# A new order table for a fused recurrent-attention and feed-forward kernel on one core

## Chip, core and metric

The kernel runs on one core of a Trainium2 chip. The metric is the time of one execution in microseconds. An order table fixes what each engine does and in which order, and the change replaces that table.

## What is computed

The inputs r, k and v have 4 batches, 8 heads, 768 positions and 48 values per head; w and u have one row per head. Everything comes in and goes out as 32-bit floats.

```
for t in range(S):
    cur     = einsum('bhd,bhe->bhde', u * k[t], v[t])
    y[t]    = einsum('bhd,bhde->bhe', r[t], state + cur)
    state   = w * state + einsum('bhd,bhe->bhde', k[t], v[t])
x   = y, heads side by side            # 3072 x 384
out = relu(x @ w_in) ** 2 @ w_out      # 384 x 2048, then 2048 x 384
```

## The kernel before

The 768 positions are cut into 6 chunks of 128, and a unit is one chunk of one batch: 24 units, numbered 0 to 23, four to a chunk. Within a chunk the recurrence is done as masked attention, and a state of 48 x 48 per head is carried from chunk to chunk. The feed-forward part then takes the 128 rows of a unit.

A unit passes through these steps. The names are those of the order table, and the line numbers are those that the profile shows.

- Loads: `rt`, `kt` (L278, or L281 for half loads) and `vt` or `vtS` (L311 on GpSimd, L309 on SyncE). Units 0 to 5 load r and k in halves of 96 KB and v on GpSimd's queue; from unit 6 on, one load of 384 KB serves two units and all are on SyncE's queue.
- `scale` (L301, L303, VectorE) multiplies r and k by powers of w into the tile rkw. `vb` (L316, L318, ScalarE) casts v.
- The transposes of r and k: up to unit 5, `turn` on TensorE (L333) and `rkT` on ScalarE (L337); from unit 6 on, `rkD` (L322), one transpose by DMA on SyncE for two units. `kb` and `kbT` (L345, L349) turn k back for the state in the first units.
- `rk` (L357, L360), `d` (L389) and `dv` (L420) make the diagonal part with u. `at` (L369) makes r times k, and `mask` (L377) evicts it. `s` (L398, L410), `sadd` (L424), `sdec` (L428) and `stb` (L432) carry the state.
- `y` (L441, L447) and `yb` (L456) make the rows of y. Up to unit 5 `xturn` and `xT` (L477, L481) transpose them for the feed-forward part, from unit 6 on `xD` (L467), a transpose by DMA on SyncE for two units.
- `m1` (L493), `relu` (L501), the squares `sqA` (L508, ScalarE) or `sqD` (L510, VectorE), `m2` in quarters (L517, and L533 in halves for unit 23), `osb` (L524) and the store `out` (L553, L549) are the feed-forward part. Units 0 to 5 do m1 in four steps of 12 matmuls; from unit 6 on a pair of units does it in eight steps of 6 wider matmuls.

The weights come in quarters on GpSimd's queue, `I` (L288) and `O` (L291). `ids`, `upper`, `zeros`, `uwb` and `wend` are small jobs of GpSimd; `wend` waits for `end` on ScalarE. `lnat`, `log`, `w`, `wk`, `wr`, `cols` and `copied` prepare the powers of w. `fill.N` is N warm-up matmuls (L216) that compute nothing that is used.

The tile framework schedules nothing itself here. The string ORDER is walked word by word, and each word emits one step into the queues of the engines that it uses. Each engine and each DMA queue then works through its own words in this order and waits, at the head of the queue, for what the next one needs. The number behind @ is the bank of PSUM that the step's result takes.

```python
for word in ORDER.split():
    what, _, where = word.partition("@")
    name, *a = what.split(".")
    ...
    if where:
        place.update(zip(names(name, *a), (int(x) for x in where)))
    steps[name](*a)
```

SyncE issues every load of r and k but one, v from unit 6 on, both kinds of DMA transposes and all stores, one behind the other.

Of the kernel before, what the change touches and what calls it, by code (L numbers as in the profile page):

```python
# [22 lines left out]
scale.3.0 relu.0.3 wend xturn.1@7 rk.2 at.2@26 xT.1 kb.2@0 mask.2.1 sqA.0.0 kt.5.0 d.2@4 turn.3.0@3 vt.3 s.0@7  # L23
sadd.1 rkT.3.0 m1.0.2@1 kt.5.1 scale.3.1 kbT.2 O.0 m1.1.0@6 mask.2.0 vb.2 relu.0.2 vt.4 turn.3.1@3 dv.2 m1.1.3@5
rt.6 rkT.3.1 sadd.0 O.1 y.2@1 relu.1.0 kt.6 m1.1.2@0 yb.2 relu.1.3 vt.5 at.3@72 rk.3 relu.1.2 kb.3@4 mask.3.1
xturn.2@6 sqA.1.0 O.2 m1.0.1@5 scale.4.0 xT.2 s.2@0 O.3 sqD.0.3 d.3@2 relu.0.1 m1.1.1@1 vb.3 mask.3.0 turn.4.0@3
kbT.3 m1.2.0@6 scale.4.1 relu.1.1 dv.3 m1.2.1@4 rkT.4.0 sqD.1.3 sqA.0.2 y.3@7 m1.2.2@1 scale.5.0 relu.2.1 sqD.1.1
m1.2.3@2 relu.2.2 sqD.0.1 s.3@5 sqA.1.2 turn.4.1@4 m2.0.0@3 sadd.3 relu.2.3 sadd.2 m2.1.0@1 rkT.4.1 yb.3 relu.2.0
m2.1.1 rk.4 vb.4 scale.5.1 kb.4@7 stb.1 xturn.3@6 at.4@42 kbT.4 m2.0.1 mask.4.1 xT.3 stb.0 s.4@5 mask.4.0 turn.5.0@6
m1.3.0@2 sqD.2.1 rkT.5.0 y.4@0 dv.4 relu.3.0 turn.5.1@6 rt.8 sadd.4 m1.3.3@7 rkT.5.1 yb.4 m2.1.2 sqA.3.0 sqA.2.0  # L30
m2.0.2 kt.8 xturn.4@2 m2.0.3 xT.4 scale.6.0 kb.5@5 osb.0 m2.1.3 scale.7.0 relu.3.3 m1.3.1@2 vtS.6 kbT.5 vb.5
m1.4.0@6 scale.6.1 scale.7.1 at.5@75 relu.4.0 m2.2.0@0 mask.5.0 osb.1 rkD.6 sqA.4.0 m1.4.1@4 sqD.2.3 sqA.2.2 sqD.3.3
m1.4.2@1 relu.3.1 mask.5.1 m2.2.1 stb.3 sdec.4 m1.4.3@6 relu.4.2 rt.10 rk.5 y.5@5 sqA.4.2 scale.8.0 s.5@2 scale.8.1
relu.4.1 m2.2.2 scale.9.0 relu.4.3 vtS.8 m1.3.2@1 sqD.3.1 stb.4 m2.3.0@4 dv.5 relu.3.2 yb.5 m2.2.3 scale.9.1 kt.10
m2.3.1 osb.2 sadd.5 sqA.4.1 m2.4.0@1 sqD.4.3 vb.6 xturn.5@0 sdec.5 at.6@2376 xT.5 rk.6 rkD.8 m2.4.1 stb.2 mask.7.0
stb.5 m1.5.0@0 sqA.3.2 mask.6.0 s.7@7 relu.5.0 mask.7.1 m1.5.3@5 mask.6.1 s.6@2 relu.5.3 m2.4.2 dv.6 out.0 vb.8
y.6@3 dv.7 rt.12 y.7@0 yb.6 m1.5.1@6 yb.7 m2.3.2 sadd.6 relu.5.1 xD.6 scale.10.0 m2.4.3 sqA.5.0 scale.10.1 sqA.5.1
m2.3.3 sadd.7 vtS.10 osb.4 m1.5.2@6 scale.11.1 scale.11.0 m2.5.0@3 relu.5.2 sqD.5.3 kt.12 m2.5.1 sqA.5.2 rk.8
at.8@1520 osb.3 sdec.6 m2.5.2 mask.9.0 rkD.10 m2.5.3 mask.8.0 s.8@4 mask.8.1 osb.5 s.9@2 m1.6.0@7 mask.9.1 m1.6.1@6
sadd.8 relu.6.0 dv.9 kt.14 m1.6.3@5 relu.6.1 dv.8 m1.6.7@1 sqA.6.0 scale.12.0 sadd.9 sqA.6.1 y.9@3 rt.14 y.8@4 vb.10  # L40
m1.6.2@0 yb.8 stb.6 m1.6.5@2 yb.9 relu.6.3 sdec.9 xD.8 m1.6.4@6 relu.6.5 scale.12.1 m2.7.0@3 relu.6.2 sqD.6.3
relu.6.7 vtS.12 m2.6.0@4 scale.13.0 relu.6.4 scale.13.1 m1.6.6@7 sqA.6.2 rk.10 at.10@6120 sqA.6.4 rkD.12 m2.6.1
relu.6.6 mask.10.0 sqA.6.5 s.10@5 sdec.7 m2.7.1 sqA.6.6 sqD.6.7 m2.7.2 stb.7 mask.10.1 stb.9 out.1 m2.7.3 sadd.10
kt.16 mask.11.0 y.10@6 osb.7 m1.8.0@1 dv.10 m1.8.1@2 rt.16 scale.14.0 relu.8.0 sdec.8 m1.8.3@5 relu.8.1 mask.11.1
m2.6.2 stb.8 yb.10 sqA.8.1 s.11@3 y.11@2 relu.8.3 dv.11 m1.8.6@1 vb.12 yb.11 m1.8.4@6 relu.8.6 sadd.11 xD.10 m2.6.3
rk.12 sqA.8.0 relu.8.4 scale.15.0 m1.8.2@2 scale.14.1 m1.8.5@0 relu.8.2 sdec.10 out.4 m2.9.0@7 osb.6 scale.15.1
vtS.14 sqA.8.2 sqD.8.3 m2.8.0@6 relu.8.5 out.3 at.12@4312 sqA.8.6 rkD.14 s.12@0 sqA.8.5 mask.13.0 m2.8.1 sqA.8.4
mask.12.1 m1.8.7@5 mask.12.0 m1.10.1@1 relu.8.7 mask.13.1 out.2 m1.10.3@3 relu.10.1 scale.16.0 vtS.16 s.13@4 sadd.12
y.12@2 dv.12 rt.18 m2.8.2 sdec.11 m1.10.6@5 yb.12 m1.10.5@0 dv.13 relu.10.6 sqD.8.7 y.13@2 stb.10 m2.9.1 relu.10.5
scale.17.0 yb.13 sqA.10.6 m2.8.3 sadd.13 relu.10.3 xD.12 m1.10.2@0 osb.8 sqD.10.3 sqA.10.1 m1.10.0@3 scale.16.1  # L50
kt.18 m1.10.7@1 relu.10.0 scale.17.1 rt.20 at.14@5642 relu.10.2 rk.14 sqA.10.0 m2.9.2 mask.15.1 vb.14 m2.9.3
mask.14.0 rkD.16 relu.10.7 m1.10.4@2 mask.14.1 sqA.10.2 mask.15.0 s.15@5 stb.11 s.14@0 sqA.10.5 m2.11.0@3 dv.14
osb.9 y.14@4 relu.10.4 y.15@6 kt.20 yb.14 vb.16 m2.11.1 sdec.12 sqA.10.4 m2.10.0@1 sadd.15 stb.12 out.5 dv.15
m1.12.0@2 sqD.10.7 m1.12.1@7 relu.12.0 yb.15 m1.12.3@4 scale.18.0 xD.14 scale.18.1 m2.10.1 relu.12.3 scale.19.0
m1.12.7@6 relu.12.1 rt.22 m2.10.2 relu.12.7 out.7 m1.12.2@7 sqA.12.0 vtS.18 sqD.12.7 m2.11.2 sdec.13 relu.12.2
scale.20.0 m1.12.6@2 sqA.12.1 kt.22 sadd.14 m1.12.4@7 scale.19.1 m1.12.5@4 scale.21.0 relu.12.4 scale.20.1 m2.11.3
relu.12.5 sqD.12.3 m2.13.0@6 sqA.12.4 rk.16 rkD.18 osb.11 at.16@4705 scale.21.1 sqA.12.2 m2.10.3 mask.16.1 relu.12.6
m1.14.7@3 sdec.15 osb.10 scale.22.0 stb.13 m2.13.1 sqA.12.5 mask.16.0 m1.14.0@7 out.10 relu.14.7 mask.17.0 out.6
s.16@2 relu.14.0 scale.23.0 m2.13.2 out.8 sqA.12.6 mask.17.1 s.17@4 rkD.20 m1.14.2@7 dv.16 sadd.16 m2.12.0@0
relu.14.2 sadd.17 m2.13.3 sdec.14 m2.12.1 dv.17 osb.13 stb.15 y.16@1 out.13 vb.18 y.17@7 yb.16 m1.14.1@6 yb.17  # L60
m2.12.2 scale.22.1 relu.14.1 xD.16 sqD.14.7 m2.12.3 sqA.14.1 scale.23.1 m1.14.6@3 sqA.14.0 rk.18 vtS.20 m1.14.3@1
relu.14.6 rkD.22 at.18@6725 osb.12 stb.14 s.18@4 mask.18.1 sqA.14.2 m1.14.5@3 relu.14.3 mask.19.0 m2.15.0@0
relu.14.5 sqD.14.3 m1.14.4@7 sqA.14.5 mask.18.0 vtS.22 m2.14.0@3 relu.14.4 dv.18 out.9 m2.15.1 mask.19.1 sqA.14.4
s.19@7 sqA.14.6 rk.20 m2.14.1 sdec.17 y.19@1 dv.19 stb.17 y.18@2 m2.14.2 yb.18 m1.16.0@6 yb.19 sadd.19 xD.18
m1.16.4@2 relu.16.0 sdec.16 m2.14.3 sadd.18 relu.16.4 out.11 m1.16.1@1 osb.14 vb.20 at.20@7256 m1.16.3@4 sqA.16.4
mask.20.1 stb.16 m1.16.2@3 rk.22 relu.16.3 m2.15.2 mask.21.1 relu.16.1 relu.16.2 s.20@4 m2.15.3 dv.20 sqA.16.1
m1.16.5@1 mask.20.0 sqA.16.2 sdec.18 m1.16.7@2 sqA.16.0 mask.21.0 relu.16.5 s.21@7 m1.18.7@6 sdec.19 relu.16.7
s.22@3 sqD.16.3 m1.18.3@1 sqA.16.5 osb.15 m1.18.1@2 vb.22 y.20@4 relu.18.1 m1.16.6@0 yb.20 relu.18.3 y.21@5 dv.21
relu.16.6 m1.18.4@4 sqD.16.7 stb.18 m2.17.0@1 yb.21 relu.18.4 dv.22 m2.16.0@0 xD.20 relu.18.7 sqA.18.1 m2.17.1
sqA.16.6 at.22@3567 out.12 out.15 m1.18.6@4 mask.22.0 out.14 m1.18.2@2 mask.22.1 relu.18.6 m2.17.2 mask.23.0  # L70
relu.18.2 mask.23.1 m2.16.1 stb.19 sqD.18.7 y.22@4 m2.16.2 s.23@2 m1.18.5@7 dv.23 m1.18.0@5 sqD.18.3 yb.22 m2.16.3
relu.18.0 m1.20.0@3 sqA.18.4 relu.18.5 m1.20.3@5 osb.16 m1.20.6@2 relu.20.3 out.16 y.23@6 sqA.18.0 sqD.20.3 m2.17.3
sqA.18.5 yb.23 m1.20.7@4 sqA.18.6 xD.22 sqA.18.2 m1.20.1@7 relu.20.7 m1.20.5@5 relu.20.0 sqD.20.7 m2.18.0@0
relu.20.6 m2.18.1 relu.20.5 sqA.20.6 m2.18.2 sqA.20.0 m2.19.0@5 m2.19.1 m1.20.2@4 m1.20.4@3 relu.20.2 m1.22.6@6
sqA.20.2 m1.22.3@4 relu.20.1 relu.20.4 m2.19.2 osb.17 m2.18.3 sqA.20.5 relu.22.6 m1.22.1@3 relu.22.3 m1.22.0@2
sqA.20.1 sqD.22.3 m2.19.3 relu.22.0 m1.22.7@1 osb.19 sqA.22.0 m2.21.0@2 sqA.20.4 m2.21.1 relu.22.1 m1.22.2@7
# [546 lines left out]
```

## Time and profile before

| what | value |
| --- | --- |
| median of 3 runs | 171.85 us (170.75 to 172.5) |
| the profiled execution | 171.94 us |
| its span | 170.2 us, 4733 instructions |
| busy: TensorE, VectorE, ScalarE, GpSimd | 163.9, 122.3, 129.8, 15.7 us |
| DMA | 28.86 MB, mean 170 GB/s |
| granted TensorE clock, mean | 0.988 |

The span runs from the first instruction to the last, and the execution's own time holds 1.7 us more. A row of the groups gives a line, an engine, an operation, output and inputs, the count, busy time, the mean of one in ns and the idle time before them. In rows by time the first number is the start in us from the beginning of the span, the second the length. In the rows by stretch each engine's busy us and instruction count are followed by the granted clock, the mean busy share of the 16 DMA engines (it can pass 1, since their packets overlap) and GB/s. A row of one step's line on SyncE gives the shortest, median and longest hold of the queue in ns and the first and last start; the row below it gives the time from issue to landing.

### The profile page before, as it was taken

To read this page: it belongs to the slowest core of one execution; us is meant where nothing else is said; L and a number is where in the kernel's file an instruction comes from. 1 tells how busy PE (TensorE), PEld (TensorE's weight loads), DVE (VectorE), ACT (ScalarE), POOL (GpSimd) and SP (SyncE) were. 2 spreads that over 40 slices of the span, in tenths; PEclk is the share of its full clock that TensorE was granted. 3 is DMA by queue.
4 is the path that set the end of the run, shared out by engine and by line. 5 is a ranking of instruction groups with operands and counts; after the bars stand their busy time and mean duration, and the time that the engine had idled before them with its cause. 6 is when DMAs were issued, how large, how long until landed. Compare 5 with 4: busy or idle time off the path is not lost.

```text
span 170.2 us, 4733 instructions
## 1 busy us (share of the span) xinstructions
PE 163.9 (96%) x1947; PEld 134.1 (79%) x1947; DVE 122.3 (72%) x243; ACT 129.8 (76%) x255; POOL 15.7 (9%) x36
## 2 busy tenths in 40 slices
...
PEclk9996999999999999999999999999999999999999
DMA  3999999999999899999999997998990501100044
GB/s 92 172 279 240 272 194 254 213 201 227 185 181 218 153 214 190 181 212 191 236 182 202 174 251 173 188 288 197 180 232 4 179 6 54 42 0 4 0 164 162
DMA packets 91493, 28.86 MB, mean 170 GB/s; under 512 B 82864, under 2 KB 90672, under 8 KB 91472
## 3 DMA queue, kind: packets, MB, share of 16 engines
...
q10 hardware_dynamic: 432, 0.25, 0.6%
...
HBM read 20.50 MB, written 4.72 MB: 148 GB/s over the span
## 4 chain that ended last, share of the span: by engine, by line
PE 87%; DMA 6%; DVE 3%; SPq 2%; issue 1%; DVEq 0%
PE bank L493 36%; PE bank L517 34%; DMA rt<-in_r_dram 4%; PE bank L369 4%; PE bank L441 3%; DMA xT<-yb 2%; PE bank L398 2%; PE bank L447 2%; SPq L281 2%; PE bank L533 2%; PE bank L333 1%; PE bank L410 1%; PE bank L345 1%; PE bank L216 1%; PE bank L477 1%
## 5 line engine op out<-in xcount | busy, mean ns | idle before, releaser
L493 PE MATMUL bank<-xT,w_in_q 128*128 128x256 bf16 (+1 forms) x720 | 72.6, 251 | 0.1
L501 ACT ACTIVATE gr<-bank 128x512 f32<-128x512 f32 x96 | 55.3, 604 | 19.0 <-PE bank L493 15.2
L517 PE MATMUL bank<-w_out_q,g 128*128 128x384 bf16 x368 | 68.6, 326 | 0.0
L493 PEld LDWEIGHTS <-w_in_q 128*128 128x128 bf16 x720 | 63.8, 113 | 3.9 <-DMA xT<-yb 0.3
L517 PEld LDWEIGHTS <-g 128*128 128x128 bf16 x368 | 34.3, 98 | 18.1 <-issue 0.2
L508 ACT ACTIVATE g<-gr 128x512 bf16<-128x512 f32 x68 | 41.2, 636 | 0.2
L377 DVE TENSOR_TENSOR am<-bank,smask 128x512 bf16<-128x512 f32 x48 | 31.3, 684 | 7.4 <-PE bank L369 6.6
L510 DVE TENSOR_TENSOR g<-gr 128x512 bf16<-128x512 f32 x28 | 19.0, 686 | 17.2 <-ACT gr L501 17.2
L524 ACT COPY osb<-bank 128x384 f32<-128x384 f32 x23 | 11.0, 480 | 5.7 <-PE bank L517 5.6
L456 DVE TENSOR_TENSOR yb<-bank,dv 128x384 bf16<-128x384 f32 x24 | 12.9, 553 | 3.2 <-PE bank L447 2.3
L420 DVE TENSOR_TENSOR dv<-vb,bank 128x384 f32<-128x384 bf16 x24 | 13.0, 548 | 2.2 <-PE bank L410 1.4
L432 ACT CAST stb<-st 128x384 bf16<-128x384 f32 x20 | 10.2, 522 | 0.6 <-DVE st L428 0.6
L301 DVE TENSOR_TENSOR rkw<-rt,wpos 128x384 bf16<-128x384 f32 x18 | 9.8, 551 | 0.8 <-DMA rt<-in_r_dram 0.7
L301 DVE TENSOR_TENSOR rkw<-kt,wneg 128x384 bf16<-128x384 f32 x18 | 9.7, 551 | 0.8 <-DMA kt<-in_k_dram 0.8
L337 ACT COPY rkT<-bank 128x512 bf16<-128x512 bf16 x12 | 7.0, 590 | 3.4 <-PE bank L333 3.4
L216 PE MATMUL bank<-warm 128*128 128x128 bf16 x87 | 8.4, 265 | 1.1 <-DVE warm L161 1.1
L441 PE MATMUL bank<-vb,am 128*128 128x48 bf16 x192 | 8.9, 185 | 0.0
L428 DVE TENSOR_TENSOR st<-st,wend 128x384 f32<-128x384 f32 x16 | 8.8, 550 | 0.0
L424 DVE TENSOR_TENSOR st<-bank,st 128x384 f32<-128x384 f32 x16 | 8.7, 549 | 0.0
L441 PEld LDWEIGHTS <-am 128*128 128x128 bf16 x192 | 7.9, 97 | 0.8
L369 PE MATMUL bank<-rkT 64*128 64x128 bf16 x192 | 8.2, 221 | 0.2 <-ACT rkT L337 0.2
L216 PEld LDWEIGHTS <-warm 128*128 128x128 bf16 x87 | 7.0, 121 | 1.2 <-DVE warm L161 1.0
...
## 6 DMA issues: line engine op xcount, KB each, us to landing
...
```

The costliest lines, as they stand in the source:

```text
L216: nc.tensor.matmul(out=banks[0][:, :128], lhsT=warm, rhs=warm, start=True, stop=True)
L301: nc.vector.tensor_tensor(t["rkw"][:, x, :, :, :D], pair(src), pair(wneg if x else wpos), ALU.mult)
L369: nc.tensor.matmul(out=t["at"][o][:, p, :], lhsT=t["rkT"][sl, 1, p, :], rhs=t["rkT"][sl, 0, p, :], start=True, stop=True,)
L377: nc.vector.tensor_tensor(am, t["at"][o], smask.unsqueeze(1).to_broadcast([C, HP, C]), ALU.mult)
L420: nc.vector.tensor_tensor(t["dv"], t["vb"], t["d"].unsqueeze(2).to_broadcast([C, H, D]), ALU.mult)
L441: nc.tensor.matmul(out=y[:, 2 * p + o, :], lhsT=t[f"am{o}"][:, p, :], rhs=t["vb"][:, 2 * p + o, :], start=(o == 0 and p == 0), stop=c == 0 ...
L456: nc.vector.tensor_tensor(t["yb"], t["y"], t["dv"].rearrange("p h d -> p (h d)"), ALU.add)
L493: nc.tensor.matmul(out=t["h", s][:, a], lhsT=turned, rhs=chunks[c]["xT"][:, b : b + m, n, :], start=(n == 0), stop=(n == NK - 1),)
L501: nc.scalar.activation(t["gr", s], t["h", s], AF.Relu)
L508: nc.scalar.activation(g, x, AF.Square)
L510: nc.vector.tensor_tensor(g, x, x, ALU.mult)
L517: nc.tensor.matmul(out=t["o"], lhsT=chunks[units[i][0]]["g"][:, f, units[i][1], :], rhs=w_out_q[f // 4][:, f % 4, :], start=(f == 0), stop ...
```

## The change

Only the string ORDER differs. Both lists hold the same steps, 882 words with the fills; the sum of the fills is 93 in the place of 87. Nearly every word is moved, over the whole span, and nearly every bank number is another. The table was searched again with a planner that takes, for how long a transpose by DMA holds SyncE, the times in the trace. The beginning and the end of the diff:

```diff
-kt.0.0 kt.0.1 rt.0.0 rt.1.0 I.0 rt.1.1 vt.0 ktA.1.0 lnat.0 fill.26 log@4567 kt.1.1 lnat.1 ids rt.2.0 w.1 upper w.0
-fill.8 cols@1 rt.2.1 wk scale.0.0 kt.2.0 zeros scale.0.1 wr fill.8 turn.0.0@2 kt.2.1 copied uwb turn.0.1@5 rkT.0.0
-rt.3.0 rkT.0.1 vt.1 rk.0 fill.10 at.0@63 scale.1.0 rt.3.1 I.3 kb.0@4 mask.0.0 d.0@2 turn.1.0@7 I.2 kbT.0 kt.3.0
-mask.0.1 rkT.1.0 vt.2 scale.1.1 vb.0 I.1 kt.3.1 fill.19 turn.1.1@4 dv.0 y.0@3 rkT.1.1 rt.4.0 yb.0 vb.1 rk.1 fill.9
-kb.1@4 kt.4.0 scale.2.0 at.1@31 xturn.0@6 rt.4.1 mask.1.1 d.1@5 turn.2.0@2 xT.0 rkT.2.0 scale.2.1 kt.4.1 fill.5
-m1.0.0@7 kbT.1 mask.1.0 turn.2.1@2 relu.0.0 dv.1 rt.5.0 fill.2 y.1@1 rkT.2.1 m1.0.3@4 yb.1 end rt.5.1 s.1@5
...
+kt.0.0 kt.0.1 rt.0.0 rt.1.0 I.0 rt.1.1 ids ktA.1.0 lnat.0 fill.26 log@4567 kt.1.1 vt.0 lnat.1 rt.2.0 w.1 upper w.0
+rt.2.1 wk scale.0.0 kt.2.0 zeros scale.0.1 wr fill.20 turn.0.0@1 kt.2.1 cols@3 rkT.0.0 turn.0.1@6 copied uwb rkT.0.1
+kt.3.0 rk.0 I.3 fill.9 at.0@32 kb.0@5 rt.3.0 vt.1 mask.0.1 d.0@6 scale.1.0 vt.2 mask.0.0 fill.14 turn.1.0@2 rt.3.1
+I.2 vb.0 kt.3.1 scale.1.1 rkT.1.0 I.1 fill.13 y.0@1 kt.4.0 dv.0 kbT.0 fill.1 turn.1.1@3 vt.3 yb.0 rt.4.0 rkT.1.1 end
+scale.2.0 fill.9 xturn.0@2 O.0 at.1@43 kt.4.1 xT.0 rk.1 fill.1 turn.2.0@1 mask.1.1 vt.4 d.1@6 m1.0.0@2 rkT.2.0
+rt.4.1 scale.2.1 O.1 mask.1.0 m1.0.3@5 vb.1 kt.5.0 relu.0.0 turn.2.1@1 dv.1 wend y.1@7 vb.2 kb.1@0 kt.5.1 yb.1 s.0@4
...
-m2.23.0@0 out.20 m2.22.3 out.19 osb.23.0 out.17 m2.23.1@1 osb.22 out.23.0 out.22 osb.23.1 out.23.1
...
+m2.22.3 m2.23.1@4 osb.22 out.22 osb.23.1 out.23.1
```

SyncE's queue from unit 6 on, taken out of the two tables:

```
before: rt.6 kt.6 rt.8 kt.8 vtS.6 rkD.6 rt.10 vtS.8 kt.10 rkD.8 out.0 rt.12 xD.6 vtS.10 kt.12 rkD.10 kt.14 rt.14 xD.8
        vtS.12 rkD.12 out.1 kt.16 rt.16 xD.10 out.4 vtS.14 out.3 rkD.14 out.2 vtS.16 rt.18 xD.12 kt.18 rt.20 rkD.16
        kt.20 out.5 xD.14 rt.22 out.7 vtS.18 kt.22 rkD.18 out.10 out.6 out.8 rkD.20 out.13 xD.16 ...
after:  rt.6 kt.6 kt.8 rt.8 out.0 vtS.6 rkD.6 rt.10 kt.10 rkD.8 vtS.8 rt.12 out.1 xD.6 kt.12 vtS.10 rkD.10 rt.14 xD.8
        out.2 vtS.12 out.5 kt.14 rkD.12 rt.16 vtS.14 xD.10 kt.16 rkD.14 vtS.16 kt.18 xD.12 rt.18 kt.20 out.4 rkD.16
        rt.20 vtS.18 xD.14 rt.22 out.3 out.7 kt.22 rkD.18 out.6 rkD.20 xD.16 ...
```

Around the first m1 step of each chunk of the middle, TensorE's words are also set otherwise: between at.16 and the end, for one, the new list has 41 paired m1 steps and 48 quarters of m2, the old one 40 and 44.

GpSimd's queue begins `I.0 ids vt.0` in the place of `I.0 vt.0 ids`, has I.3 ahead of vt.1, and has wend behind O.1 and no longer ahead of vt.3. ScalarE has vb.0 ahead of rkT.1.0, and end ahead of xT.0.

More of the change, by code (lines that the diff above doesn't have):

```diff
@@ L22 @@
-m1.0.0@7 kbT.1 mask.1.0 turn.2.1@2 relu.0.0 dv.1 rt.5.0 fill.2 y.1@1 rkT.2.1 m1.0.3@4 yb.1 end rt.5.1 s.1@5
[L23 to L76, printed above, removed]
@@ new lines @@
+kt.3.0 rk.0 I.3 fill.9 at.0@32 kb.0@5 rt.3.0 vt.1 mask.0.1 d.0@6 scale.1.0 vt.2 mask.0.0 fill.14 turn.1.0@2 rt.3.1
+I.2 vb.0 kt.3.1 scale.1.1 rkT.1.0 I.1 fill.13 y.0@1 kt.4.0 dv.0 kbT.0 fill.1 turn.1.1@3 vt.3 yb.0 rt.4.0 rkT.1.1 end
+scale.2.0 fill.9 xturn.0@2 O.0 at.1@43 kt.4.1 xT.0 rk.1 fill.1 turn.2.0@1 mask.1.1 vt.4 d.1@6 m1.0.0@2 rkT.2.0
+rt.4.1 scale.2.1 O.1 mask.1.0 m1.0.3@5 vb.1 kt.5.0 relu.0.0 turn.2.1@1 dv.1 wend y.1@7 vb.2 kb.1@0 kt.5.1 yb.1 s.0@4
+rkT.2.1 vt.5 sadd.0 kbT.1 xturn.1@3 rt.5.0 kb.2@1 rk.2 xT.1 at.2@62 scale.3.0 O.3 kbT.2 mask.2.1 m1.1.0@3 relu.0.3
@@ new lines @@
+rt.5.1 mask.2.0 m1.1.3@1 O.2 relu.1.0 scale.3.1 y.2@2 sqA.1.0 rt.6 d.2@7 turn.3.0@5 dv.2 s.1@4 m1.0.2@0 rkT.3.0
+sadd.1 kt.6 relu.1.3 turn.3.1@7 yb.2 m1.1.2@3 relu.0.2 xturn.2@6 s.2@2 m1.0.1@1 xT.2 scale.4.0 rkT.3.1 m1.2.0@0
+sqD.0.3 sqA.0.0 sadd.2 at.3@65 sqA.0.2 turn.4.0@4 sqD.1.3 relu.1.2 m1.1.1@7 rk.3 relu.0.1 m1.2.1@2 mask.3.1 relu.2.0
+scale.4.1 m1.2.3@1 rkT.4.0 mask.3.0 relu.2.1 m2.0.0@3 sqD.0.1 vb.3 turn.4.1@5 kb.3@6 rkT.4.1 d.3@0 y.3@2 m2.1.0@4
+dv.3 relu.1.1 yb.3 kb.4@5 kbT.3 m1.2.2@0 scale.5.1 sqA.1.2 sqD.1.1 at.4@76 relu.2.3 xturn.3@2 kbT.4 scale.5.0 m2.0.1
@@ new lines @@
+xT.3 mask.4.0 m2.1.1 stb.0 mask.4.1 relu.2.2 turn.5.0@1 turn.5.1@2 vb.4 rk.4 m1.3.1@7 rkT.5.0 y.4@6 kt.8 vb.5 s.4@5
+relu.3.1 s.3@1 m1.3.2@0 sadd.4 sqA.2.0 sadd.3 m2.1.2 relu.3.2 dv.4 rt.8 m2.1.3 rkT.5.1 sqD.2.1 stb.3 m2.0.2 rk.5
+sqA.2.2 yb.4 m2.0.3 stb.1 scale.6.0 xturn.4@0 scale.7.0 m1.3.3@7 osb.0 xT.4 out.0 kb.5@1 scale.6.1 stb.2 m2.2.0@3
+kbT.5 vtS.6 scale.7.1 at.5@25 m1.3.0@1 rkD.6 mask.5.0 m2.2.1 sqD.3.1 relu.3.0 sqD.2.3 m2.2.2 relu.3.3 osb.1 mask.5.1
+s.5@0 sqA.3.0 m1.4.0@2 sadd.5 m1.4.1@1 scale.8.0 relu.4.0 rt.10 scale.8.1 y.5@6 relu.4.1 dv.5 m1.4.3@5 scale.9.0
```

47 lines of the change are left out of this document (45 added, 2 removed).

## The prediction

> **What bounds the kernel now.** I read the page first, then busy time by stretch, then the table of waits, then the chain that ended last, and last SyncE's issues one by one.
>
> ```profile
> PE 163.9 (96%) x1947; PEld 134.1 (79%) x1947; DVE 122.3 (72%) x243; ACT 129.8 (76%) x255; POOL 15.7 (9%) x36
> ...
> PEclk9996999999999999999999999999999999999999
> DMA  3999999999999899999999997998990501100044
> GB/s 92 172 279 240 272 194 254 213 201 227 185 181 218 153 214 190 181 212 191 236 182 202 174 251 173 188 288 197 180 232 4 179 6 54 42 0 4 0 164 162
> ```
>
> Two resources are full at once: TensorE in every slice after the start, and the DMA engines in nearly every slice from the second to the thirtieth (about 126 us). The stretches say it more sharply:
>
> ```profile
> 10.00:20.00 10.00, 9.05 (x148) 8.29 (x149) 8.60 (x17) 6.20 (x15) 3.10 (x6) 0.83 1.15 244
> 70.00:80.00 10.00, 10.00 (x122) 8.41 (x121) 8.59 (x17) 8.88 (x17) 0.00 (x0) 1.00 1.01 204
> ```
>
> TensorE loses time before 20 us alone: it idles 0.95 us of that stretch and its granted clock is 0.83. At 70 to 80 us it is busy throughout, beside a DMA share of 1.01. The table of waits has only scraps for TensorE after the start:
>
> ```profile
> POOL wend L268 <- ACT wend_c L263: 6.9, 1, 6.9
> ...
> PEld L493 <- DMA xT<-yb: 0.3, 1, 0.3
> ...
> PEld L369 <- DMA rkT<-rkw: 0.2, 1, 0.2
> ```
> ```profile
> L322 SPq DMA_TRANSPOSE rkT<-rkw x9: 2171/3824/4443, 38.5 to 117.5; - x9
> ```
>
> So a transpose never held TensorE up for more than 0.3 us, though each rkD holds SyncE for 2.2 to 4.4 us (min, median and max in the last row): what the new order was searched for costs TensorE next to nothing in the old one. The chain gives the price of each TensorE step and the end:
>
> ```profile
> 76.81 3.79 DMA xT<-yb
> 80.65 1.50 PE bank L493 x12
> ...
> 91.35 0.19 PE bank L398 x4
> 91.54 0.65 PE bank L517 x4
> 92.19 0.20 PE bank L441 x8
> 92.39 0.17 PE bank L447 x4
> ...
> 102.72 0.55 PE bank L369 x16
> ...
> 143.16 1.97 PE bank L493 x18
> ...
> 166.43 0.91 PE bank L533 x16
> ```
>
> A paired m1 step (6 matmuls) costs 0.66 us, an m2 quarter 0.65, a y step 0.37 (8 and 4 matmuls), an s step a little over 0.19; at.16 starts at 102.7. The last matmul ends at 167.3; 2.9 us of last eviction and store close the span, and 1.7 us lie outside it (171.94 for this execution, 0.1 above the median of the runs). The chain passes through one transfer behind a full TensorE: xD.10, issued at 76.81, landed at 80.6, and m1.10.1 started with it.
>
> **What the change can touch.** It adds no instruction but six warm-up matmuls (93 for 87):
>
> ```profile
> L216 PE MATMUL bank<-warm 128*128 128x128 bf16 x87 | 8.4, 265 | 1.1 <-DVE warm L161 1.1
> ```
>
> Six of them are 0.6 us at that row's rate. All stand ahead of m1.0.0, where TensorE waits for loads and evictions, so I cost them at nothing; without that cover it is the 0.6. Everything else is moved, on all five queues. With TensorE full after the start, a new order can win only at the start, and it loses wherever TensorE comes to ask for a transfer sooner than the DMA engines bring it.
>
> **The start.** TensorE, VectorE, ScalarE and GpSimd, in turn:
>
> ```profile
> 10.74 0.40 PE L333 MATMUL bank<-identb,rkw 128*128 128x128 bf16 x4 [1.84 <-DVE rkw L303]
> ...
> 16.26 0.83 PE L493 MATMUL bank<-xT,w_in_q 128*128 128x128 bf16 x12
> ```
> ```profile
> 10.13 0.56 DVE L303 TENSOR_TENSOR rkw<-rt,wfour 128x384 bf16<-128x384 f32 x1 [1.63 <-DMA rt<-in_r_dram]
> 10.60 1.28 DVE L377 TENSOR_TENSOR am<-bank,smask 128x512 bf16<-128x512 f32 x2
> ...
> 13.37 0.56 DVE L456 TENSOR_TENSOR yb<-bank,dv 128x384 bf16<-128x384 f32 x1 [0.56 <-PE bank L441]
> ```
> ```profile
> 11.18 0.59 ACT L337 COPY rkT<-bank 128x512 bf16<-128x512 bf16 x1 [1.84 <-PE bank L333]
> 11.66 0.52 ACT L318 CAST vb<-vt 128x384 bf16<-128x384 f32 x1
> 13.05 0.59 ACT L337 COPY rkT<-bank 128x512 bf16<-128x512 bf16 x1 [0.88 <-PE bank L333]
> ...
> 15.73 0.48 ACT L481 COPY xT<-bank 128x384 bf16<-128x384 bf16 x1 [1.68 <-PE bank L477]
> ```
> ```profile
> 3.72 0.96 POOL L311 DMA_DIRECT2D vt<-in_v_dram  x1
> ...
> 18.61 0.99 POOL L268 COPY wend<-wend_c 64x192 f32<-64x192 f32 x2 [6.86 <-ACT wend_c L263]
> ```
>
> The load that both orders wait for (scale.1.0 starts at 10.13) is not moved. Of the two masks that followed it the new list does mask.0.1 inside the 1.63 us wait, so mask.0.0 ends 0.6 us sooner. Against that, vt.0 goes behind the identities on GpSimd, about 0.9 us, and vb.0 now stands ahead of rkT.1.0 on ScalarE: rkT.1.0, kbT.0 and rkT.1.1 queue behind that load, and at.1 waits for the first and the last. vt.0 was there by 11.66. Its landing moves by 0 to 0.9 us; it follows I.0 through the same queue in both orders, so I take none and put vb.0 at 11.6 to 12.1. Then, with the durations above, rkT.1.0 ends at 12.7, kbT.0 at 13.2, rkT.1.1 at 13.8, y.0 at 12.5, dv.0 and yb.0 at 13.6, xturn.0 at 14.0 (the list now puts it ahead of at.1, and moves kb.1 behind m1.0.0), and xT.0, behind two small activations of 0.4, at 14.7. That is the lower bound for m1.0.0, all on time. The upper one is 15.9: turn.1.1 to d.1 took from 12.40 to 16.26 at the low clock, less the 0.4 by which kb.1 goes. I take the middle, **15.3, 1.0 us early**; by m1.1.0 about 0.4 of it is gone again, because vb.1, vb.2 and relu.0.0 (0.5 to 0.6 each) now stand ahead of xT.1 on ScalarE. TensorE's own end moves from 167.3 to **166.7**, with bounds of 165.7 and 167.3.
>
> By the Trainium skill (TensorE: Matmul & The Clock Gate, Part 1: The HAM clock gate) the array runs at half clock by default and after an idle window of some 3.4 us, at full clock after a busy one. The 0.83 above agrees with a gate of that kind. If the 14 fills that now stand ahead of turn.1.0 keep that window busy, this rule would give the early bound, an end near 165.7, in place of 166.7.
>
> **The transfers.** SyncE's rkD.6, rkD.8, rkD.10 and rkD.16, each with its issue and its time to landing, and the xD group:
>
> ```profile
> L322 SPq DMA_TRANSPOSE rkT<-rkw x1: 4115/4115/4115, 38.5 to 38.5; - x1
> DMA to landing us min/median/max: 5.5/5.5/5.5
> ...
> L322 SPq DMA_TRANSPOSE rkT<-rkw x1: 3600/3600/3600, 48.0 to 48.0; - x1
> DMA to landing us min/median/max: 5.1/5.1/5.1
> ...
> L322 SPq DMA_TRANSPOSE rkT<-rkw x1: 4443/4443/4443, 58.3 to 58.3; - x1
> DMA to landing us min/median/max: 7.7/7.7/7.7
> ...
> L322 SPq DMA_TRANSPOSE rkT<-rkw x1: 3824/3824/3824, 93.4 to 93.4; - x1
> DMA to landing us min/median/max: 6.6/6.6/6.6
> ```
> ```profile
> L467 SPq DMA_TRANSPOSE xT<-yb x9: 1211/1262/3002, 53.0 to 143.3; - x9
> ```
>
> They land at 44.0, 53.1, 66.0 and 100.0. An xD that nothing holds up costs 1.2 us (min and median of its row); an rkD turns 16 blocks to its 6, so 3.2. Between the first two landings stand three loads and one rkD: 9.1 less 3.2 leaves 2.0 for a load of 384 KB. A store has 192 KB, so at most 1.0; at the best slice of the page's last row (288 GB/s) it would be 0.7, which I take, since its rows are long. As a test, from 44.0 to xD.10 the old queue has 11 loads, 3 rkD, 3 xD and 2 stores: 22.0 + 9.6 + 3.6 + 1.4 = 36.6, so 80.6, which is where it landed. The transfers are a chain as full as TensorE's, and what is put ahead of a transpose delays it by its price.
>
> Now the new queue. Up to xD.10 it has the same 11 loads (kt.16 is moved behind it, vtS.14 ahead), the same transposes, but four stores: out.0 ahead of vtS.6 and rkD.6, then out.1, out.2 and out.5, where the old one had out.0 and out.1. That is 2 x 0.7 = 1.4 more: xD.10 lands at 82.0. TensorE needs it for m1.10.1, which stood 86.7 us ahead of the end (80.65 to 167.3); behind it the new list has the same 56 m1 steps, 57 m2 quarters and 5 at, one y and one s fewer, 0.6 us: 86.1. **So the end is 82.0 + 86.1 = 168.1**, and m1.10.1, ready at 166.7 - 86.1 = 80.6, waits 1.4 us. A second place says nearly the same: up to rkD.16 both queues have 16 loads and 5 stores, so it still lands at 100.0, but at.16 now has 4 m2 quarters and one m1 step more behind it, 64.6 + 3.3 = 67.9, and 100.0 + 67.9 = 167.9. The other transposes have 0.5 us or more to spare by the same count (rkD.8 and rkD.12 over a microsecond in the old order), and vtS.8, moved behind rkD.8, delays the cast vb.8 but not past s.9. Outer bounds: at 1.0 a store the end is 168.7; if a queue of this kind runs ahead of the sum, TensorE's 166.7 stands.
>
> **Sum.** 168.1 for 167.3 is 0.7 to 0.8 us on the span; with the tail and the time outside unchanged, 171.94 + 0.7 = **172.6 us**, 0.8 above the median shown and inside the 1% that a measurement of this kernel can tell from no change (its three runs lie 1.0% apart).
>
> **The rivals.**
> - *The transfers give way, the start's gain stays* (faster). The holds of SyncE leave gaps in the DMA engines, which an order that knows them may close; the wait at m1.10.1 goes and the end is TensorE's own 166.7: 171.3, at the early bound 170.3. For it: the late transposes of the old run (rkD.20 on) are not needed at once. Against: the share of 1.01 in the middle.
> - *xD.10 lags behind its sum* (slower). rkD.10 landed at 66.0, where the sum (44.0 + 6 loads, 2 rkD, one xD, one store = 20.3) gives 64.3: 1.7 late, and nobody waited but for 0.2 us. With the slack now spent, the same lag on xD.10 or rkD.16 goes to the end in full: 83.7 + 86.1 = 169.8, or 174.4. It makes the run slower by over 1% from a lag of 1.0 us on.
> - *GpSimd's queue crowds out SyncE's loads* (slower). wend moves behind O.1, and end to before xT.0, so the 6.9 us in which GpSimd waited go, and vt.3, O.0, vt.4 and O.1 are issued from about 12 instead of 19.6. The share of 1.15 says that the DMA engines are full there, so the half loads of units 4 and 5 lose what GpSimd gains. If they come 3.4 us later, half of the 6.9, and 1.4 of it is covered, turn.4.0 and turn.5.0 wait 2.0: 168.7, or 173.3; with all of it, 176.8. By the Trainium skill (DMA: Bandwidth & Descriptors, Queues, rings and completion order) each DMA engine takes turns between the queues that have work, packet by packet, which speaks for this loss; no row above separates the two queues.
>
> **How the numbers follow.** The forecast (172.0 to 173.4) has 0.42, the faster rival 0.20, the lag 0.26, the crowding 0.12. Over 1% slower (173.6 on) are the lag, half of the crowding and the top of the forecast's own spread: 0.40. Over 1% faster (170.1 or less) needs the early bound and no wait at all: 0.06. The rest, 0.54, is within 1%. The range leaves out the fastest of the second case and the worst of the last two: 171.0 to 175.0.
>
> **What would show it.** Right: m1.0.0 starts near 15.3; TensorE has its first wait of over a microsecond for xT<-yb near 81 us, or for rkT<-rkw near 100; the page's chain has DMA in it there; VectorE and ScalarE totals stay. The step on the start is wrong if m1.0.0 starts after 16.3 or before 14.7; the step on the stores, if xD.10 lands before 81 with its four stores ahead; the crowding shows as TensorE waits between 22 and 33 us on rkw L303. A run under 170.5 or over 175 would mean that neither chain is what sets the end.

## The result and the profile after

The changed table takes 173.42 us in the median of 12 runs (172.09 to 177.53), the old one 171.20 (170.66 to 172.50): a ratio of 1.011, with an interval of 1.008 to 1.014. The profiled execution took 172.73 us with a span of 170.9, 0.7 more than the span of before. Ratios here and below leave out the executions that lie over 1.5% above the fastest of their kernel.

The page of after, the rows that answer to those of before, and under them busy time by stretch:

```profile
PE 163.0 (95%) x1953; PEld 132.9 (78%) x1953; DVE 122.1 (71%) x243; ACT 130.2 (76%) x255; POOL 15.5 (9%) x36
...
PEclk9999999999999999999999999999999999999999
DMA  3999999989998999999999999999980236002023
...
PE 71%; DMA 13%; ACT 5%; SPq 3%; POOL 2%; issue 1%; DVE 1%; ACTq 1%; DVEq 0%
```
```profile
10.00:20.00 10.00, 8.35 (x149) 7.21 (x150) 8.48 (x18) 7.63 (x18) 7.28 (x11) 1.00 1.14 230
20.00:30.00 10.00, 9.77 (x175) 8.82 (x173) 8.12 (x17) 8.97 (x19) 0.55 (x1) 1.00 1.10 250
70.00:80.00 10.00, 10.00 (x124) 8.14 (x123) 9.13 (x18) 9.31 (x19) 0.00 (x0) 1.00 1.04 213
120.00:130.00 10.00, 9.36 (x107) 7.49 (x106) 6.73 (x13) 7.47 (x15) 0.00 (x0) 1.00 0.72 148
```

The granted clock is listed as full from the start (0.83 at 10 to 20 us before). The middle is as full as it was. TensorE stands idle 1.65 us at 10 to 20, 0.23 at 20 to 30 and 0.64 at 120 to 130, where the DMA share is only 0.72. So the wait forecast near 81 us is not there, and two others are. The first, in TensorE's rows by time:

```profile
13.30 0.84 PE L493 MATMUL bank<-xT,w_in_q 128*128 128x128 bf16 x12
14.46 0.86 PE L493 MATMUL bank<-xT,w_in_q 128*128 128x128 bf16 x12 [0.32 <-DMA w_in_q<-in_moe_w_in_dram]
...
16.11 0.36 PE L441 MATMUL bank<-vb,am 128*128 128x48 bf16 x8 [0.56 <-ACT vb L318]
...
17.36 0.34 PE L477 MATMUL bank<-identb,yb 128*128 128x128 bf16 x3 [0.50 <-DVE yb L456]
...
22.82 1.36 PE L493 MATMUL bank<-xT,w_in_q 128*128 128x128 bf16 x21 [0.23 <-DMA w_in_q<-in_moe_w_in_dram]
```

m1.0.0 starts at 13.3 where it started at 16.3. A way to follow such a lead is to add to the start of a TensorE step the work that still stands behind it in the list, at the durations of the prediction's rows: the end if TensorE never waited again. The old run stands at 167.1 from 15 us on. The new one stands at 164.6 at xturn.0, and then gives all of it back: 0.5 at m1.0.3 (the weights I.3), 0.7 at y.1 (vb.1, cast from vt.1), 0.7 at xturn.1 (yb.1, behind y.1), 0.2 at y.2 and 0.4 at m1.0.1 (the weights I.1). From m1.0.1 it stands at 167.2, where the old run stands.

The second wait, in SyncE's, ScalarE's and TensorE's rows by time:

```profile
116.09 0.45 SPq L309 DMA_DIRECT2D vt<-in_v_dram  x1
116.59 3.86 SPq L553 DMA_DIRECT2D out_dram<-osb  x3
120.49 0.43 SPq L309 DMA_DIRECT2D vt<-in_v_dram  x1
```
```profile
124.56 0.83 ACT L316 CAST vb<-vt 128x768 bf16<-128x768 f32 x1 [1.31 <-DMA vt<-in_v_dram]
125.30 0.51 ACT L432 CAST stb<-st 128x384 bf16<-128x384 f32 x1
125.72 0.59 ACT L501 ACTIVATE gr<-bank 128x512 f32<-128x512 f32 x1
126.21 0.46 ACT L524 COPY osb<-bank 128x384 f32<-128x384 f32 x1
```
```profile
125.86 0.33 PE L447 MATMUL bank<-stb,rkT 128*128 128x96 bf16 x4 [0.20 <-ACT stb L432]
...
126.72 0.82 PE L493 MATMUL bank<-xT,w_in_q 128*128 128x256 bf16 x6 [0.45 <-ACT osb L524]
```

The stores out.8, out.9 and out.10 hold SyncE for 3.86 us, so vtS.22 is issued at 120.5 and lands at 124.5. ScalarE, which takes its words in order, stands at vb.22 for 1.31 us. Nobody needs vb.22 then, but stb.16, relu.16.7 and osb.14 stand behind it, and y.20 and m1.16.5 wait for these. By the same working the end moves here from 167.5 to 168.0; the 0.3 since m1.0.1 are not traced to single waits.

And the transpose of the forecast, with rkD.16 (SyncE's lines in windows around one issue):

```profile
L467 SPq DMA_TRANSPOSE xT<-yb x1: 2111/2111/2111, 76.8 to 76.8; - x1
...
DMA to landing us min/median/max: 3.9/3.9/3.9
...
L322 SPq DMA_TRANSPOSE rkT<-rkw x1: 2642/2642/2642, 93.4 to 93.4; - x1
...
DMA to landing us min/median/max: 5.5/5.5/5.5
```

xD.10, with its four stores ahead, lands at 80.7 and not 82.0; m1.10.1 starts at 80.8 without a wait. rkD.16 lands at 98.9 and not 100.0.

One thing of after is off without a wait of TensorE behind it in this execution. The last half loads of unit 5, before and after, and GpSimd's rows of after:

```profile
L281 SPq DMA_DIRECT2D rt<-in_r_dram x1: 534/534/534, 17.1 to 17.1; - x1
...
DMA to landing us min/median/max: 4.4/5.1/5.8
```
```profile
L281 SPq DMA_DIRECT2D rt<-in_r_dram x2: 534/534/534, 16.4 to 18.2; - x2
...
DMA to landing us min/median/max: 12.0/12.1/12.1
```
```profile
12.28 0.92 POOL L311 DMA_DIRECT2D vt<-in_v_dram  x1
13.19 0.56 POOL L291 DMA_DIRECT2D w_out_q<-in_moe_w_out_dram  x1
```

From issue to landing the two of after (rt.5.0 and rt.5.1) take 12.0 us, the last three of before (rt.5.1, kt.5.0 and kt.5.1) 4.4 to 5.8; unit 5 has all its data at 30.2 us in the place of 23.8. Unit 4 is not late here: rt.4.1 lands at 22.4, before at 22.2. vt.3 and O.0, which stood behind the 6.9 us of wend, now go out from 12.3 us on.

### The profile page after: what moved, and what is told of

It reads as the page before. It is cut to its first block, busy times and chain, and to the rows that moved or that the text cites. A ratio compares the mean times of both kernels' runs of the same rounds, so it can differ in the third digit from the quotient of the medians.

```text
span 170.9 us, 4748 instructions
## 1 busy us (share of the span) xinstructions
PE 163.0 (95%) x1953; PEld 132.9 (78%) x1953; DVE 122.1 (71%) x243; ACT 130.2 (76%) x255; POOL 15.5 (9%) x36
## 4 chain that ended last, share of the span: by engine, by line
PE 71%; DMA 13%; ACT 5%; SPq 3%; POOL 2%; issue 1%; DVE 1%; ACTq 1%; DVEq 0%
PE bank L517 31%; PE bank L493 29%; DMA w_in_q<-in_moe_w_in_dram 7%; DMA rkT<-rkw 5%; PE bank L369 3%; SPq L553 3%; DMA vt<-in_v_dram 2%; PE bank L441 2%; ACT gr L501 2%; PE bank L533 2%; PE bank L447 2%; PE bank L398 1%; ACT g L508 1%; POOL vt L311 1%; POOL w_in_q L288 1%
## 5 line engine op out<-in xcount | busy, mean ns | idle before, releaser
L493 PE MATMUL bank<-xT,w_in_q 128*128 128x256 bf16 (+1 forms) x720 | 73.7, 252 | 1.0 <-DMA w_in_q<-in_moe_w_in_dram 0.5
L517 PE MATMUL bank<-w_out_q,g 128*128 128x384 bf16 x368 | 69.3, 326 | 0.0
L493 PEld LDWEIGHTS <-w_in_q 128*128 128x128 bf16 x720 | 63.6, 113 | 5.5 <-DMA w_in_q<-in_moe_w_in_dram 0.8
L216 PE MATMUL bank<-warm 128*128 128x128 bf16 x93 | 7.8, 245 | 1.1 <-DVE warm L161 1.1
L316 ACT CAST vb<-vt 128x768 bf16<-128x768 f32 x9 | 7.5, 834 | 1.5 <-DMA vt<-in_v_dram 1.5
L369 PEld LDWEIGHTS <-rkT 64*128 64x128 bf16 x192 | 5.4, 94 | 3.6 <-issue 1.7
```

The lines of the kernel that those rows point to most:

```text
L369: nc.tensor.matmul(out=t["at"][o][:, p, :], lhsT=t["rkT"][sl, 1, p, :], rhs=t["rkT"][sl, 0, p, :], start=True, stop=True,)
L493: nc.tensor.matmul(out=t["h", s][:, a], lhsT=turned, rhs=chunks[c]["xT"][:, b : b + m, n, :], start=(n == 0), stop=(n == NK - 1),)
L517: nc.tensor.matmul(out=t["o"], lhsT=chunks[units[i][0]]["g"][:, f, units[i][1], :], rhs=w_out_q[f // 4][:, f % 4, :], start=(f == 0), stop ...
```

## The experiments

The edits are words of ORDER that move; "after" and "before" name the table that is edited. The first four kernels have a line less in the table, so their line numbers are one lower (L492 is L493).

### Three stores behind rkD.22 (e1_a_late)

```diff
 after
-m1.14.4 out.8 sqA.14.1 mask.19.0 out.9 ... mask.18.1 out.10
+at.20 rkD.22 out.8 out.9 out.10 vb.20
```

> The new table with out.8, out.9 and out.10 moved from ahead of vtS.22 to behind rkD.22 in SyncE's queue; nothing else. Theory (stores ahead of loads on SyncE): vtS.22 is issued some 3.5 us sooner (near 117 instead of 120.5), vb.22 on ScalarE no longer waits 1.3 us, and the 0.9 us that TensorE loses at 125 to 127 us go: about 0.9 us less than the new table, near 172.5 by the median. Rival (the loss comes from the start, where TensorE waits for weights and v from GpSimd's queue): no change, within 0.3 us of the new table.

172.17 us, 1.0049 (1.0008 to 1.0089). vtS.22 lands at 119.0. The stretch from 120 us and vb.22 on ScalarE:

```profile
120.00:130.00 10.00, 10.00 (x116) 8.32 (x111) 6.07 (x11) 8.40 (x17) 0.00 (x0) 1.00 0.48 119
```
```profile
120.19 0.84 ACT L315 CAST vb<-vt 128x768 bf16<-128x768 f32 x1
```

vb.22 has no wait in brackets and TensorE no idle time. The late wait comes from the place of these stores. By the medians about half of the loss goes with it, though the ten executions spread from 170.78 to 174.25 and the profiled one, 170.88, is among the fastest.

### Two stores behind rkD.14 (e2_a_mid), and both edits (e3_a_both)

```diff
 after
-relu.6.7 out.2 sdec.9 ... relu.6.5 out.5 scale.13.1
+sdec.10 rkD.14 out.2 out.5 relu.8.5
```

> The new table with out.2 and out.5 moved from ahead of rkD.12 to behind rkD.14. Theory with the prediction's price of 0.7 us a store: rkD.12, xD.10 and rkD.14 land 1.4 us sooner (near 75.6, 79.3 and 85.9), the wait of 0.3 us at at.14 goes, and the run is 0.3 us shorter than the new table. Rival (a store costs the transposes nothing, because SyncE's holds leave gaps): the landings stay within 0.5 us and the wait stays.

173.60 us, 1.0142 (1.0075 to 1.0208). xD.10 lands at 79.4 (1.3 earlier) and rkD.14 at 84.7 (2.6 earlier), but at.16 waits 0.5 us instead, and the late wait remains. The landings follow the stores; the time does not follow these landings.

> Both moves of stores together in the new table. Theory: the two gains add up to 1.2 us against the new table, and since TensorE is then at the old table's pace from 24 us on, the time is that of the old table within 0.3 us. Rival (other waits come up in their place, because the transfers are late everywhere): less than half of that, still 0.6 us or more above the old table.

173.64 us, from 171.14 to 176.31. The ratio, 1.0040 (0.9993 to 1.0087), rests on the faster half of these ten executions and says too little; with the stores behind rkD.22 alone the median was 172.17. Nothing is to be had from the two middle stores.

The landings give a price for these two: behind xD.8, xD.10 lands 12.1 to 13.0 us later in after and the seven other tables made from it that keep the stores there, 11.4 in e2 and 12.0 in e3. From the mean of the eight, 12.5, that is some 0.2 to 0.5 us a store.

### The disputed price in the old table (e4_b_two)

```diff
 before
-relu.8.6 sadd.11 xD.10 ... sdec.10 out.4 ... relu.8.5 out.3
+relu.8.6 sadd.11 out.4 out.3 xD.10
```

> The old table with out.4 and out.3 moved from behind xD.10 to ahead of it; nothing else. Theory of the prediction: two stores at 0.7 us put xD.10 1.4 us later, near 82.0, m1.10.1 waits 1.4 us for it, and the run is 1.2 to 1.4 us longer than the old table. Rival (the stores fill gaps that SyncE's holds leave): xD.10 lands less than 0.7 us later and the run is within 0.7 us of the old table.

171.64 us, 1.0028 (0.9985 to 1.0071). xD.10 and m1.10.1:

```profile
L466 SPq DMA_TRANSPOSE xT<-yb x1: 1220/1220/1220, 77.2 to 77.2; - x1
...
DMA to landing us min/median/max: 2.9/2.9/2.9
```
```profile
80.17 1.07 PE L492 MATMUL bank<-xT,w_in_q 128*128 128x256 bf16 x8 [0.46 <-DMA xT<-yb]
```

rkD.12 landed at 73.0, so xD.10 came 7.1 us after it, against 6.5 in the profile of before and 6.2 and 6.4 in e7 and e11, further down, which leave this stretch as it was: two stores cost 0.6 to 0.9 us, **0.3 to 0.45 each, not 0.7**. The wait that the forecast rested on does exist (0.5 here, m1.10.1 behind xD.10), but at less than half of its size.

### Without 27 fills (e5_a_nofill)

```diff
 after
-mask.0.0 fill.14 turn.1.0 ... I.1 fill.13 y.0
+mask.0.0 turn.1.0 ... I.1 y.0
```

> The new table without its fill.14 and fill.13 (27 warm-up matmuls fewer, around turn.1.0). Theory (what sets TensorE's pace by 24 us is the arrival of I.3, vt.1 and I.1 on GpSimd's queue, so the early start is lost again): m1.0.0 starts later, by 0.5 to 2 us, if the clock drops in the place of the fills; the waits at m1.0.3, y.1 and m1.0.1 shrink by about as much; the time stays that of the new table within 0.5 us. Rival (the start counts in full): the run is longer by what m1.0.0 is late, 1 us or more.

174.27 us, 1.0125 (1.0081 to 1.0170). In its profiled execution TensorE idles where the fills were, and m1.0.0 comes at the same time as after:

```profile
10.28 0.40 PE L333 MATMUL bank<-identb,rkw 128*128 128x128 bf16 x4 [0.91 <-DVE rkw L303]
11.19 0.36 PE L441 MATMUL bank<-vb,am 128*128 128x48 bf16 x8 [0.51 <-ACT vb L318]
...
13.47 0.73 PE L493 MATMUL bank<-xT,w_in_q 128*128 128x128 bf16 x10
```

That profile alone says that the fills do nothing. The mean granted clock, which is listed for every execution, says otherwise:

| kernels | executions | mean clock 0.99 or less | median at 0.997 or more | median at 0.99 or less |
| --- | --- | --- | --- | --- |
| table before | 89 (without one of 420 us) | 29 | 170.81 | 171.66 |
| nine tables from after, with the fills | 82 | 4 | | |
| after without 27 fills (e5) | 10 | 7 | 172.90 | 174.97 |

A mean of 0.99 is what one slice of the forty at 0.6 makes; the profile of before has 0.988, with its one slice of 6 at 13 to 17 us. The other tables with the fills that ran on e5's chip (e6 and e8) have 1 in 22. So the fills do hold the clock, and the third of the old table's executions with a drop are 0.85 us slower in the median. By the Trainium skill (TensorE: Matmul & The Clock Gate, Part 1: The HAM clock gate) idle time of some 3.4 us sends the array to half clock. The counts agree in direction; the profile of before has its drop after a single wait of 1.84 us among shorter ones, so the length isn't settled here.

It follows that the two tables are compared best among executions at full clock: 173.33 (10 executions) against 170.81 (60), a difference of medians of **2.5 us** (1.8 to 2.8, resampled), not 0.7. The differences below are made so, against the old table on the same chip.

### vb.22 moved instead of the stores (e6_a_vb), and the old table spoiled (e7_b_vb)

```diff
 after
-sqA.16.0 sdec.19 vb.22 s.20
+m1.16.3 osb.14 vb.22 sqD.16.7
 before
-osb.15 m1.18.1 vb.22 y.20
+sqA.16.4 mask.20.1 vb.22 stb.16
```

> The new table with vb.22 moved on ScalarE from ahead of stb.16 to behind osb.14; the stores stay where they are. Theory (the late loss is a wait in ScalarE's order: vb.22 waits for vtS.22, and stb.16, relu.16.7 and osb.14 stand behind it): vtS.22 still lands near 124.5, but TensorE's 0.9 us at 125 to 127 us go, as they did when the stores were moved; about 0.9 us less than the new table. Rival (the stores delay the transfers as such, and moving them helped by that): no gain, within 0.3 us of the new table.

173.17 us, 1.0104 (1.0067 to 1.0141). The late wait is gone (TensorE busy 10.00 of 10.00 us from 120 on), but this execution pays elsewhere, in its table of waits:

```profile
DVE rkw L303 <- DMA rt<-in_r_dram: 4.0, 3, 2.5
...
PEld L333 <- DVE rkw L303: 2.7, 4, 1.0
```

turn.4.0, turn.5.0 and what follows them lose 1.5 us: rt.4.1 lands at 24.3 (22.4 in after) and rt.5.1 at 32.4 (30.2), and now they are waited for. At full clock the nine executions stand 2.1 us above the old table (1.2 to 2.9), so this edit shows the late wait gone and not what it is worth.

> The old table with vb.22 moved on ScalarE to ahead of stb.16, as in the new one. Theory: ScalarE stops at vb.22 until vtS.22 lands (125.8 in the old trace), stb.16 and what follows it are 2 us or more late, TensorE waits there for 1 us or more, and the old table becomes 0.6 to 2 us longer. Rival (that place has room in the old table): no change, within 0.3 us.

172.42 us, 1.0076 (1.0052 to 1.0101); at full clock 1.4 us more than before (1.2 to 1.8). ScalarE and TensorE:

```profile
123.94 0.83 ACT L316 CAST vb<-vt 128x768 bf16<-128x768 f32 x1 [1.60 <-DMA vt<-in_v_dram]
```
```profile
125.74 0.24 PE L410 MATMUL bank<-uwb,rk 128*128 128x8 bf16 x4 [1.88 <-ACT gr L501]
```

One cast put too early in ScalarE's order is enough to spoil the old table.

### GpSimd's queue held back (e9_a_gate), and let loose in the old table (e11_b_crowd)

```diff
 after
-... vt.3 ... end ... O.0 ... vt.4 ... O.1 ... wend ... vt.5 sadd.0
+rk.2 xT.1 end wend vt.3 O.0 vt.4 O.1 vt.5 at.2 ... dv.2 sadd.0
 before
-... wend ... vt.3 ... O.0 ... vt.4 ... O.1
+vb.0 I.1 vt.3 O.0 vt.4 O.1 kt.3.1 ... wend
```

> The new table with GpSimd's wait given back: end behind xT.1 on ScalarE, wend ahead of vt.3, O.0, vt.4, O.1 and vt.5 on GpSimd, and sadd.0 behind dv.2 on VectorE, since it needs wend. Theory (GpSimd's queue crowds out SyncE's half loads): GpSimd issues vt.3 near 19 instead of 12, rt.4.1 and rt.5.1 land near 22 and 23 to 25 as in the old table (22.4 and 30.2 in the trace of the new one, 24.5 and 32.7 in others), turn.4.0 and turn.5.0 wait for nothing, and the slow half of the executions goes: 0.5 us or more off the new table's median, the late 0.9 us staying. Rival (the loads of units 4 and 5 are early enough in either case): no change within 0.3 us.

172.04 us, 1.0062 (1.0027 to 1.0096).

```profile
L281 SPq DMA_DIRECT2D rt<-in_r_dram x2: 534/535/536, 17.6 to 18.7; - x2
L281 SPq DMA_DIRECT2D kt<-in_k_dram x1: 535/535/535, 16.5 to 16.5; - x1
...
DMA to landing us min/median/max: 5.0/5.7/6.1
```

The half loads take 5 to 6 us again, and nothing waits at turn.4.0 or turn.5.0. The edit has a price of its own: s.1 waits 0.9 us for sadd.0, which now frees its bank later.

> The old table with vt.3, O.0, vt.4 and O.1 moved on GpSimd from behind wend to ahead of it; nothing else. Theory (crowding): GpSimd issues them near 12 to 15 instead of 19.6 to 22; SyncE's rt.4.1, rt.5.1 and kt.5.1 land 2 to 8 us later than the 22.2, 22.9 and 23.8 of the old trace; TensorE waits at the turns of units 4 and 5, 0.5 to 2 us in all, and the run is as much longer. Rival: the loads are late and nobody waits, no change within 0.3 us.

174.39 us (4 runs), 1.0113 (1.0039 to 1.0187). SyncE's half loads, VectorE and TensorE:

```profile
L281 SPq DMA_DIRECT2D kt<-in_k_dram x2: 535/535/535, 17.8 to 18.9; - x2
...
DMA to landing us min/median/max: 12.4/13.3/13.6
```
```profile
29.31 0.56 DVE L303 TENSOR_TENSOR rkw<-rt,wfour 128x384 bf16<-128x384 f32 x1 [2.02 <-DMA rt<-in_r_dram]
```
```profile
32.53 0.38 PE L345 MATMUL bank<-identb,rkT 128*128 128x128 bf16 x4 [1.17 <-DVE yb L456]
```

The move of four GpSimd words alone makes the old table's half loads as late as after's, and VectorE and TensorE wait for them; TensorE is idle 1.4 us from 30 to 70 us. How much longer the run is by this stays open: the ratio rests on two of four executions (173.44 and 172.38; the others took 175.35 and 176.39), and this one started slowly. The same 19 warm-up matmuls, in e11 and in e4:

```profile
11.12 2.23 PE L216 MATMUL bank<-warm 128*128 128x128 bf16 x19
```
```profile
10.21 1.22 PE L215 MATMUL bank<-warm 128*128 128x128 bf16 x19
```

At nearly twice the time for a matmul m1.0.0 came at 16.0, where e4 has 14.0; yet the clock is listed as 1.00 from 10 to 20 us and 0.998 in the mean. So a mean clock near 1 does not exclude a slow start.

### The repairs together (e8_a_best, e10_a_full, e12_a_full2)

```diff
 after, e8: stores and vb.22 moved as above, and
-I.3 ... kb.0 rt.3.0 vt.1 ... mask.1.0 m1.0.3 vb.1
+vt.1 I.3 ... yb.1 s.0 m1.0.3 rkT.2.1
 e10: stores and vb.22 moved as above, and GpSimd's queue held back
 e12: as e10, and
-s.1@4 ... xturn.2@6
+s.1@6 ... xturn.2@4
```

> The new table with four moves: the three late stores behind rkD.22, vb.22 behind osb.14, vt.1 ahead of I.3 on GpSimd, and m1.0.3 behind s.0 on TensorE. Theory: the late 0.9 us go, and at the start y.1 no longer waits for vt.1 (0.7 us) nor m1.0.3 for I.3 (0.5 us); what stays is xturn.1 (0.7) and the wait for I.1 (0.4, growing by what is gained, since I.1's landing does not move). TensorE is then 0.2 us or less behind the old table and the time is that of the old one within 0.5 us. Rival (the waits at the start hide nothing): 1 us better than the old table.

172.85 us, 1.0071 (1.0034 to 1.0109). The waits between m1.0.0 and 20 us shrink from 1.4 to 0.7, but turn.4.0 alone loses 0.8, and 1.7 go to the late half loads in all:

```profile
25.21 0.40 PE L333 MATMUL bank<-identb,rkw 128*128 128x128 bf16 x4 [0.80 <-DVE rkw L303]
```

TensorE stood ready for turn.4.0 0.2 us sooner than in after (24.4 against 24.6), and rt.4.1 landed 2.1 us later (24.5 against 22.4): most of this wait is the load's.

> The new table with GpSimd's wait given back as in the kernel before this one, and with the late repair: out.8, out.9 and out.10 behind rkD.22, vb.22 behind osb.14. Theory: both causes of the loss are gone, so the time is that of the old table within 0.3 us; it can be better by no more than 0.5, since xD.10 and rkD.16 still land when they do. Rival (a third cause): 0.5 us or more above the old table.

172.87 us, 1.0101 (1.0060 to 1.0142): s.1 waits 0.9 us for its bank, and three waits between 16 and 19 us take 1.4 more, which hides the rest.

> The kernel with both repairs once more (GpSimd's wait given back, the late stores and vb.22 moved), with s.1 in bank 6 and xturn.2 in bank 4 in the place of 4 and 6: in the last two kernels s.1 took the bank of s.0, which sadd.0, moved behind dv.2, had not yet read, and TensorE waited 0.9 to 1.0 us there. Theory (crowding and the late wait are the whole loss): that wait goes, no other of over 0.7 us comes after 24 us, and the time is that of the old table within 0.4%. Rival (a third cause): 0.5% or more above it.

172.17 us, 1.0067 (1.0038 to 1.0097); the eight executions lie within 171.70 and 172.56. No late half loads, no wait at s.1, none near 125 us. The longest wait that is left behind m1.0.0:

```profile
23.45 1.53 PE L493 MATMUL bank<-xT,w_in_q 128*128 128x128 bf16 x24 [0.95 <-DMA w_in_q<-in_moe_w_in_dram]
```

So the theory that the late cast and the half loads are the whole loss fell. The third part lies between m1.0.0 and m1.0.1. The new list has m1.0.1 due at 22.5 us here and 22.6 in after, and I.1 lands at 23.4 and 22.8. The old list at full clock (e4 and e7) has it due at 22.4 and 22.3, with I.1 there at 21.8. At full clock e12 stands 1.5 us above the old table (1.0 to 1.9); this wait is 1.0, and xturn.1 waits 0.5 for yb.1. Why I.1 lands later is not shown, and no run takes this part away. No version beat the old table.

## Why the prediction was right in its number and wrong in its place

- **The number.** 172.6 was forecast, 0.4% over the median shown, and 173.42 came, inside the range; the ratio of 1.011 is just past the 1% beyond which lay 0.40, the time just short of its 173.6. That the number fits is luck: the 1.4 us that made it did not come, and waits that were not costed stood in for them.
- **The store, 0.7.** It was worked out from the best slice's bandwidth and tested on one landing, with 2 stores among 17 other terms, which can't see it. Measured by itself it is 0.3 to 0.45 (e4), and 0.2 to 0.5 by e2 and e3. With 0.3 the forecast's own sum gives 81.2 for xD.10; it came at 80.7, and the 1.4 us at m1.10.1 were none.
- **The start, 15.3.** 13.3 came, below the lower bound of 14.7. The sum carried vb.0 at 11.6 and later (it started at 10.5), and took durations from a stretch at a clock of 0.83. The base was at fault too: the profiled execution of before was one of the third whose clock drops. In e4 and e7, at full clock, the same start has m1.0.0 at 14.0 and 14.3; 0.8 of the difference to 16.3 is there already at turn.1.0, whose load came later, and the rest comes at the low clock. The new start varies as well: 13.4 to 13.5 in e1, e2 and e3, on e4's chip, and on e7's chip 13.5 in e5 and 14.4 in e6, where vb.0 came at 11.6. So the new order is 0 to 1.0 us earlier, and the forecast's 1.0 is the top of that. Adding 0.7 to an execution of 171.94 at a low clock hid that full-clock executions lose 2.5.
- **The gain that stays.** That an end of 166.7 would follow from the start was the step that failed most: nothing behind m1.0.0 was costed for what it waits for. I.3, vt.1 and I.1 arrive when GpSimd's queue brings them, and TensorE's lead ran into them (the 2.5 us given back by 23 us, and 1.0 in e12). Against the old table at full clock it is more than a lead lost: turn.4.0 starts at 25.2 in the profile of before and at 24.1 and 23.9 in e4 and e7, so where the new run stands level with the first, it is about 1 us behind the other two.
- **The late cast.** The prediction followed the transposes on SyncE and checked vtS.8, not vtS.22. The question that it put to xD, what stands ahead of it, belonged to every load that an engine's next word waits for. It is worth 1.4 us in the old table (e7).
- **The crowding, chance 0.12.** It is real, at the place named (turn.4.0, turn.5.0) and near the size named: 2.0 us forecast, 1.5 in e6, 1.7 in e8, 1.4 on TensorE in e11. The price that it was given as a rival, 173.3, is near what came, though after's own profiled execution has the late loads without the wait. Beside the rows of e11 and e9, the Trainium skill (DMA: Bandwidth & Descriptors, Queues, rings and completion order) says that a DMA engine takes turns between the queues by packets; a SyncE load that takes 12 us and more beside GpSimd's loads, and 5 to 6 where these are held back, agrees with it.
- **The fills.** Costing their own 0.6 us at nothing was right. The rule on the clock, which the prediction kept as a side line, goes the same way: with the 14 and 13 fills the clock holds in 78 of 82 executions. The end near 165.7 that the rule was to give did not come.
- **Right as told:** no rkD wait of size (0.5 us at most at at.14 and at.16), the middle stays full, and VectorE's and ScalarE's totals stay within 0.4 us.

What stays open is how the 2.5 us divide. e1, e6, e9 and e12 each take away one part or more and end at 1.2, 2.1, 1.5 and 1.5 us above the old table on their chip, with intervals about 1 to 2 us wide, and only one execution of each has rows. The three parts overlap: a lead lost at one is not lost again at the next.
